# An exponential placed first on ScalarE, and half as many identity products in TensorE's waits

## The chip, the cores and the metric

The kernel runs on one core of one Trainium2 chip. The metric is the device time of one execution, in microseconds (us); less is better. A core has TensorE (PE: matrix products, its weight loads listed apart as PEld), VectorE (DVE), ScalarE (ACT), GpSimd (POOL) and SyncE (SP, which here issues the transfers). They run side by side and wait for each other through semaphores.

## The reference

Attention in two stages with 32 "pack" vectors for each head, then a feed-forward layer with Silu over all heads:

```
q, k, v: (8, 8, 576, 64)   p: (8, 8, 32, 64)      # batch, heads, tokens, width
sm_attn(q, k, v) = softmax(q @ k.T / 8) @ v
p_packed = sm_attn(p, k, v)
x = sm_attn(q, p_packed, p_packed)                # then (4608, 512): tokens x (head, width)
h = x @ w_in                                      # w_in (512, 2048)
out = (h * sigmoid(h)) @ w_out                    # w_out (2048, 512)
```

All is float32.

## The kernel before, in words

The feed-forward layer is computed with the packs inside: since x is (shares of the packs) times (packs), `packs @ w_in` is made first for each batch ("pp" steps), and the shares ("a2") are multiplied with it. A **unit** is one batch and one block of 128 of the 2048 hidden columns: `h` makes its products (line 521), `g` its Silu on ScalarE (539 to 542), `o` the products with w_out (557), summed up in PSUM. To keep precision, most operands are split into a high and a low part and multiplied in three products; the first four units (`u < WHOLE`) use whole float32 values instead.

The early part, until all 64 early units are done, is one list written out by hand, `ORDER`. Each word is a step, and each engine takes its part of the steps strictly in this order (PE, DVE, ACT and SP are scheduled by hand). The words that the change and the prediction touch, for batch 0 (`as0.1` is step `as` of batch 0, second half):

- `W8`: `keep_warm(8)`, line 135: eight 128x128 products of the identity `ident` with itself into a PSUM tile that nobody reads. One float32 product is two instructions on PE, so `W8` shows as x16 in the profile. They stand where PE waits for another engine or for a transfer.
- `k0`, `v0`, `q0`: transfers of the packs and keys (in two pieces), of the values, and of the queries (in two pieces); `wf0` to `wf18`: of chunks of the two weight matrices.
- `ws`, `wz`, `wj`: scaling (ACT, lines 188 and 189), sign (DVE, 193 and 194) and joining (DVE 200, then DVE or POOL 201) of the weights, which arrive as 64-bit integers that hold the bits of a number.
- first attention: `as` scores (PE, line 228), `am` largest value (DVE, 264, 265), `ax` exponentials (ACT, 274), `ar` reciprocals (DVE, 278, 279), `at` transposes (PE, 293), `ay` copies out of PSUM (DVE for the first parity, ACT for the second, 311 and 312), `aa` products with v (PE, 326), `an` (DVE, 336), `ai` (PE 345, ACT copy 349).
- `pp0` packs times w_in (PE, 228), `pu0` its copy (ACT, 486).
- second attention: `aS` scores (PE, 228), `aC` copy (ACT, 370), `aB` transposes (PE, 378), `aM` less the largest (DVE, 407, 408), `aX` exponentials (ACT, 419), `aD` shares (DVE, 428 to 431), `aU` transposes back (PE, 398 and 400), `aF` copy (ACT, 445).
- `h0.0`: the products of the first unit, first half; then `g0.0`, and so on. `as1.0`, `as1.1`, `ac1.1` (ACT, 254), `am1` belong to batch 1; `h2.0` is the third unit.

Both exponentials and Silu run on ScalarE, which loads a table when it goes from one function to the other (`ACT_TABLE_LOAD`); copies and scalings need no load of their own. `two_banks()` gives one of two PSUM tiles, in turn; the tile of the identity products is given up when the next step asks for one. After `ORDER`, a plain loop goes over the rest of the units.

In `ORDER`, the stretch from the start to the first unit reads

```
W8 k0 as0.0 W1 as0.1 am0.0 wf0 wf1 am0.1 ax0.0 ax0.1 ar0 v0 ws0 wz0 W5 at0.0 ay0.0 at0.1 ay0.1 wf2 ws1 ws2 wj0 W15
aa0 an0 W2 ai0 wz2 aj0 q0 W2 pp0 aS0.0 aC0.0 pu0 W2 aS0.1 aB0.0 aC0.1 wj2 pp1 wz1 wj1 wf3 ws3 aM0.0 aX0.0 wf4 ws4
aB0.1 aM0.1 aX0.1 aD0.0 W32 aU0.0 wf5 ws5 wf6 ws6 aD0.1 wz4 aF0.0 W4 h0.0 pu1 k1 g0.0 wz6 aU0.1 aF0.1 wj6 as1.0
```

Of the kernel before, what the change touches and what calls it, by code (L numbers as in the profile page):

```python
# [9 lines left out]
F32 = mybir.dt.float32  # L10
# [4 lines left out]
AF = mybir.ActivationFunctionType  # L15
# [4 lines left out]
P = 128  # L20
# [30 lines left out]


ORDER = """
W8 k0 as0.0 W1 as0.1 am0.0 wf0 wf1 am0.1 ax0.0 ax0.1 ar0 v0 ws0 wz0 W5 at0.0 ay0.0 at0.1 ay0.1 wf2 ws1 ws2 wj0 W15
aa0 an0 W2 ai0 wz2 aj0 q0 W2 pp0 aS0.0 aC0.0 pu0 W2 aS0.1 aB0.0 aC0.1 wj2 pp1 wz1 wj1 wf3 ws3 aM0.0 aX0.0 wf4 ws4
aB0.1 aM0.1 aX0.1 aD0.0 W32 aU0.0 wf5 ws5 wf6 ws6 aD0.1 wz4 aF0.0 W4 h0.0 pu1 k1 g0.0 wz6 aU0.1 aF0.1 wj6 as1.0
ac1.0 wu1 h1.0 g1.0 wf7 wf8 aH0.1 wz5 h0.1 g0.1 h1.1 ws7 v1 wz3 as1.1 wj3 ac1.1 wj5 wj4 g1.1 am1 o0.0 ax1.0 ax1.1
pp3 wz7 wj7 wf9 pp2 pu2 o1.0 at1.0 at1.1 pu3 o0.1 h2.0 h2.1 ws8 g2.0 g2.1 ws9 aL0.1 wz8 o1.1 h3.0 h3.1 wf10 ws10 wj8
o2.0 wz9 aH0.0 wj9 wz10 wj10 g3.0 g3.1 wf11 ws11 o2.1 pp4 aL0.0 o3.0 ay1 aa1 pu4 pl4 h4 wu5 wu10 g4 ar1 an1 ai1 wl1
# [24 lines left out]
def packed_attention_ffn(ctx: ExitStack, tc: tile.TileContext, pkT, qT, v, w_in, w_out, out):  # L84
# [13 lines left out]
    nc = tc.nc  # L98
    ent = ctx.enter_context
    const = ent(tc.tile_pool(name="const", bufs=1))  # L100
# [10 lines left out]
    ident = const.tile([P, P], F32, name="ident")  # L111
# [4 lines left out]

    rest = const.tile([P, NF, 2, 2, REST], F32, name="rest")
    parts = tc.dram_tile((EARLY, 2, P, 2, DM), F32, name="parts")

    made = {}  # L120

# [662 lines left out]
```

## Time and profile before

| | |
|---|---|
| device time, median of 3 runs | 713.53 us (713.42 to 713.99) |
| profiled execution | 713.74 us, span 711.8 us |
| PE busy | 700.6 us (98%), 5126 products |
| DVE, ACT, POOL busy | 332.5 us (47%), 328.3 us (46%), 20.9 us (3%) |
| products of the identity (line 135) | 142 instructions, 19.6 us busy (pipelined, so with overlap) |
| table loads on ACT | 16 under line 539 (20.5 us) and 2 under line 274 up to 60 us, 1283 ns each |
| HBM | 85 GB/s over the span; 356 GB/s in its first fortieth |

The span goes from the first to the last instruction of the execution; the device time has some 2 us more around it. In a line of the timeline the first number is the start in us from the start of the span, the second the time that the group took, then engine, line, operation, the tiles (written <- read), shapes and count; in square brackets stands how long the engine was idle before, and what ended that. In a list of transfers the last number is the median time from issue to landing in us.

### The profile page before, as it was taken

Reading aid. Unit: us, or ns where it says so; the run is one execution under the profiler, and the core shown is the slowest. Engines: PE = TensorE matmul, PEld = TensorE weight load, DVE = VectorE, ACT = ScalarE, POOL = GpSimd, SP = SyncE. Lnnn points to the kernel's source line nnn. Section 1 sums busy time; section 2 is a strip of 40 time slices with the busy share of each in tenths; the row PEclk is TensorE's granted clock in tenths of the full one; section 3 lists DMA queues with packets and bytes.
Section 4 is the critical chain, followed back from the end, with each engine's and each line's share of the span. In section 5 each row is a group of like instructions: output and inputs, shape, how many; then the busy total and the mean of one; then the engine's idle time right before and its main releaser. Section 6 shows DMA issues by size and latency. Waiting matters only on the chain.

```text
span 711.8 us, 12233 instructions
## 1 busy us (share of the span) xinstructions
PE 700.6 (98%) x5126; PEld 570.4 (80%) x5126; DVE 332.5 (47%) x491; ACT 328.3 (46%) x613; POOL 20.9 (3%) x16
## 2 busy tenths in 40 slices
PE   8999999999999999999999999999999999999997
PEld 6756778887868887888878888878878888888886
DVE  3979985854643336331562325533362334622112
ACT  3696867733534425362542625453352532533221
POOL 0112011110000000000000000000000000000000
PEclk9999999999999999999999999999999999999999
DMA  9765572425032140212211122021401210010002
GB/s 356 295 201 196 191 255 101 164 68 192 1 130 82 34 145 1 105 39 87 75 60 56 43 89 75 22 104 36 145 1 60 81 36 1 1 60 1 1 0 75
DMA packets 30870, 65.21 MB, mean 92 GB/s; under 512 B 19296, under 2 KB 19296, under 8 KB 26464
## 3 DMA queue, kind: packets, MB, share of 16 engines
q1 hardware_dynamic: 30720, 64.30, 25.6%
q8 instruction: 41, 0.67, 0.4%
q10 hardware_dynamic: 96, 0.13, 0.1%
q14 instruction: 13, 0.11, 0.0%
HBM read 48.76 MB, written 11.53 MB: 85 GB/s over the span
## 4 chain that ended last, share of the span: by engine, by line
PE 96%; ACT 1%; DVE 1%; SPq 0%; DMA 0%; issue 0%; POOL 0%; ACTq 0%; POOLq 0%; DVEq 0%
PE ps_acc L557 56%; PE ps_two L521 28%; PE ps_two L228 6%; PE ps_two L135 2%; PE ps_two L326 2%; SPq L305 0%; PE ps_acc L228 0%; ACT tm L274 0%; DVE mx L264 0%; ACT L274 0%; DMA tm<-tm 0%; PE ps_acc L326 0%; ACT pw_hi L486 0%; PE ps_acc L293 0%; PE ps_acc L378 0%
## 5 line engine op out<-in xcount | busy, mean ns | idle before, releaser
L557 PE MATMUL ps_acc<-wo_hi,g_hi 128*128 128x512 f32 x560 | 222.5, 397 | 0.0
L557 PE MATMUL ps_acc<-wo_lo,g_hi 128*128 128x512 f32 x560 | 219.1, 391 | 0.0
L557 PE MATMUL ps_acc<-wo_hi,g_lo 128*128 128x512 f32 x560 | 219.0, 391 | 0.0
L547 DVE TENSOR_TENSOR g_lo<-g,g_hi 128x512 fp32r<-128x512 f32 x124 | 89.2, 720 | 256.6 <-ACT g_hi L541 256.5
L539 ACT ACTIVATE g<-ps_two 128x512 f32<-128x512 f32 x124 | 74.4, 600 | 265.6 <-PE ps_two L521 236.7
L521 PE MATMUL ps_two<-a_lo,pw_hi 128*128 128x288 f32 x528 | 155.4, 303 | 0.1
L521 PE MATMUL ps_two<-a_hi,pw_hi 128*128 128x288 f32 x496 | 147.2, 297 | 1.0 <-ACT rest L542 1.0
L521 PE MATMUL ps_two<-a_hi,pw_lo 128*128 128x288 f32 x496 | 145.9, 294 | 0.0
L557 PEld LDWEIGHTS ps_acc<-wo_hi,g_hi 128*128 128x128 f32 x560 | 105.1, 188 | 38.8 <-issue 19.4
L557 PEld LDWEIGHTS ps_acc<-wo_hi,g_lo 128*128 128x128 f32 x560 | 105.1, 188 | 23.6 <-DVE g_lo L547 0.7
L557 PEld LDWEIGHTS ps_acc<-wo_lo,g_hi 128*128 128x128 f32 x560 | 105.2, 188 | 18.1
L521 PEld LDWEIGHTS ps_two<-a_lo,pw_hi 128*128 128x128 f32 x528 | 98.9, 188 | 6.6 <-ACT rest L542 0.8
L521 PEld LDWEIGHTS ps_two<-a_hi,pw_hi 128*128 128x128 f32 x496 | 93.3, 188 | 5.7 <-ACT rest L542 1.3
L521 PEld LDWEIGHTS ps_two<-a_hi,pw_lo 128*128 128x128 f32 x496 | 93.2, 188 | 0.0
L541 ACT ACTIVATE g_hi<-ps_two 128x512 fp32r<-128x512 f32 x124 | 73.6, 593 | 7.8 <-PE ps_acc L557 7.8
L489 DVE TENSOR_TENSOR pw_lo<-ps_two,pw_hi 128x1024 fp32r<-128x1024 f32 x31 | 36.8, 1220 | 9.4 <-ACT pw_hi L486 9.4
L486 ACT CAST pw_hi<-ps_two 128x1024 fp32r<-128x1024 f32 x31 | 30.2, 1017 | 15.9 <-PE ps_two L228 15.9
L228 PE MATMUL ps_two<-win,ppT 64*32 64x512 f32 (+1 forms) x560 | 32.4, 559 | 2.4 <-DVE pw_lo L489 1.6
L542 ACT ACTIVATE rest<-ps_two 128x64 f32<-128x64 f32 (+1 forms) x132 | 30.1, 228 | 0.0
L228 PEld LDWEIGHTS ps_two<-win,ppT 64*32 64x32 f32 x560 | 8.1, 105 | 17.4 <-issue 10.1
L539 ACT ACT_TABLE_LOAD x16 | 20.5, 1283 | 2.0 <-PE ps_two L521 1.9
L135 PE MATMUL ps_two<-ident 128*128 128x128 f32 x142 | 19.6, 296 | 1.4 <-POOL ident masks.py:199 1.4
(114 smaller groups left out, 480.6 us busy)
## 6 DMA issues: line engine op xcount, KB each, us to landing
kvq_t<-in_v SPq DMA_DIRECT2D x8, 1280.0 KB, 6.3
kvq_t<-in_pkT SPq DMA_DIRECT2D x7, 1216.0 KB, 6.3
out<-o SPq DMA_DIRECT2D x16, 512.0 KB, 2.8
kvq_t<-in_qT SPq DMA_DIRECT2D x7, 1152.0 KB, 5.1
w_raw<-in_w_in SPq DMA_DIRECT2D x6, 1024.0 KB, 5.7
win<-in_w_out SPq DMA_DIRECT2D x3, 1024.0 KB, 4.7
w_raw<-in_w_out SPq DMA_DIRECT2D x3, 1024.0 KB, 4.6
tm<-tm SPq DMA_DIRECT2D x56, 40.0 KB, 2.0
```

The source lines that it names most:

```text
L135: nc.tensor.matmul(made["warm"][:, 0, :P], ident, ident, start=True, stop=True)
L228: nc.tensor.matmul(bank(par)[NP * i : NP * i + NP], lhs(r, i), rhs(r, i), start=True, stop=True)
L326: nc.tensor.matmul(self.ps[NP * i : NP * i + NP, par * D : par * D + D], e, vs[:n, c, h * D : h * D + D], start=(c == 0), stop=(c == 4),)
L486: nc.scalar.copy(self.hi, self.ps[:, :, : self.nf * P])
L489: nc.vector.tensor_tensor(self.lo, self.ps[:, :, : self.nf * P], self.hi.bitcast(F32), ALU.subtract)
L521: nc.tensor.matmul(bank, p[:, par, cols], a[:, par], start=(n == 0), stop=(n == len(todo) - 1))
L539: nc.scalar.activation(g, ps[..., :MAIN], AF.Silu)
L541: nc.scalar.activation(g_hi, ps[..., :MAIN], AF.Silu)
L542: nc.scalar.activation(to, ps[..., MAIN:HS], AF.Silu)
L547: nc.vector.tensor_tensor(g_lo[:, c], g[:, c], g_hi[:, c].bitcast(F32), ALU.subtract)
L557: nc.tensor.matmul(bank, g[:, rows], w[:, at], start=(first and n == 0), stop=(last and n + 1 == len(todo)))
```

## The change

A tile `ready` of 128x1 is allocated, and ScalarE takes the exponential of the first column of the identity into it before anything else; no step reads `ready`. In `ORDER` the counts of the nine `W` steps go from 8, 1, 5, 15, 2, 2, 2, 32, 4 (71 products, 142 instructions) to 6, 1, 4, 7, 1, 1, 1, 15, 2 (38 products, 76 instructions). Nothing else in the order moves.

```
 ORDER = """
-W8 k0 as0.0 W1 as0.1 am0.0 wf0 wf1 am0.1 ax0.0 ax0.1 ar0 v0 ws0 wz0 W5 at0.0 ay0.0 at0.1 ay0.1 wf2 ws1 ws2 wj0 W15
-aa0 an0 W2 ai0 wz2 aj0 q0 W2 pp0 aS0.0 aC0.0 pu0 W2 aS0.1 aB0.0 aC0.1 wj2 pp1 wz1 wj1 wf3 ws3 aM0.0 aX0.0 wf4 ws4
-aB0.1 aM0.1 aX0.1 aD0.0 W32 aU0.0 wf5 ws5 wf6 ws6 aD0.1 wz4 aF0.0 W4 h0.0 pu1 k1 g0.0 wz6 aU0.1 aF0.1 wj6 as1.0
+W6 k0 as0.0 W1 as0.1 am0.0 wf0 wf1 am0.1 ax0.0 ax0.1 ar0 v0 ws0 wz0 W4 at0.0 ay0.0 at0.1 ay0.1 wf2 ws1 ws2 wj0 W7
+aa0 an0 W1 ai0 wz2 aj0 q0 W1 pp0 aS0.0 aC0.0 pu0 W1 aS0.1 aB0.0 aC0.1 wj2 pp1 wz1 wj1 wf3 ws3 aM0.0 aX0.0 wf4 ws4
+aB0.1 aM0.1 aX0.1 aD0.0 W15 aU0.0 wf5 ws5 wf6 ws6 aD0.1 wz4 aF0.0 W2 h0.0 pu1 k1 g0.0 wz6 aU0.1 aF0.1 wj6 as1.0
...
     parts = tc.dram_tile((EARLY, 2, P, 2, DM), F32, name="parts")
 
+    ready = const.tile([P, 1], F32, name="ready")
+    nc.scalar.activation(ready, ident[:, :1], AF.Exp)
+
     made = {}
```

## The prediction

> **What bounds the kernel now.** The page comes first: span, busy times, and the chain that ended last.
>
> ```profile
> span 711.8 us, 12233 instructions
> PE 700.6 (98%) x5126; PEld 570.4 (80%) x5126; DVE 332.5 (47%) x491; ACT 328.3 (46%) x613; POOL 20.9 (3%) x16
> ...
> PE 96%; ACT 1%; DVE 1%; SPq 0%; DMA 0%; issue 0%; POOL 0%; ACTq 0%; POOLq 0%; DVEq 0%
> ```
>
> PE is busy nearly always, and the chain lies on it for 96%. But part of that busy time is identity products, which no step reads. The change touches only the first 31 us, so the question is what else holds PE there. That is read from the timeline of PE (start, time taken, in brackets the wait).
>
> ```profile
> 1.36 3.78 PE L135 MATMUL ps_two<-ident 128*128 128x128 f32 x16 [1.36 <-POOL ident masks.py:199]
> 5.07 1.15 PE L228 MATMUL ps_acc<-kvq_t 64*32 64x288 f32 x16
> 6.16 0.49 PE L135 MATMUL ps_two<-ident 128*128 128x128 f32 x2
> 6.57 0.72 PE L228 MATMUL ps_acc<-kvq_t 64*32 64x288 f32 x16
> 7.22 1.38 PE L135 MATMUL ps_two<-ident 128*128 128x128 f32 x10
> 10.54 1.49 PE L293 MATMUL ps_acc<-ident,tm 128*128 128x128 f32 x10 [1.94 <-ACT tm L274]
> 11.87 3.51 PE L135 MATMUL ps_two<-ident 128*128 128x128 f32 x30
> 15.31 1.73 PE L326 MATMUL ps_acc<-kvq_t,tm 128*32 128x64 f32 x80
> ...
> 19.08 0.71 PE L135 MATMUL ps_two<-ident 128*128 128x128 f32 x4
> 19.73 0.66 PE L228 MATMUL ps_acc<-o,ppT 64*32 64x256 f32 x16
> 20.32 0.87 PE L378 MATMUL ps_acc<-ident,tm 128*128 128x128 f32 x6
> ...
> 22.00 7.31 PE L135 MATMUL ps_two<-ident 128*128 128x128 f32 x64
> 29.14 0.38 PE L398 MATMUL ps_acc<-ident,tm 128*128 128x128 f32 x2
> ...
> 30.17 1.16 PE L135 MATMUL ps_two<-ident 128*128 128x128 f32 x8
> 31.48 1.21 PE L521 MATMUL ps_two<-a_lo,pw_hi 128*128 128x288 f32 x4
> ...
> 44.00 2.10 PE L521 MATMUL ps_two<-a_lo,pw_hi 128*128 128x288 f32 x8
> ...
> 54.28 1.09 PE L228 MATMUL ps_two<-win,ppT 64*32 64x512 f32 x16 [0.83 <-DVE win L201]
> ```
>
> An identity product takes 0.24 us at first (3.78/16) and 0.12 later (3.51/30); the scores took 1.15 us and then, the same 16 products, 0.72. So PE runs at half rate until some 6.4 us (the record of the granted clock says 1.00 throughout and does not show it). Where an `L135` row has no wait behind it, the next step went when the identity products let it: only another engine's row tells when it could have gone. These are on ACT and DVE.
>
> ```profile
> 8.36 1.28 ACT L274 ACT_TABLE_LOAD   x1 [8.36 <-DVE nm L265]
> 9.65 0.74 ACT L274 ACTIVATE tm<-ps_acc,nm 128x576 f32<-128x576 f32 x1
> ...
> 10.39 0.73 ACT L274 ACTIVATE tm<-ps_acc,nm 128x576 f32<-128x576 f32 x1
> ...
> 30.81 0.38 ACT L486 COPY pw_hi<-ps_two 128x256 f32<-128x256 f32 x1
> ...
> 43.26 0.62 ACT L486 COPY pw_hi<-ps_two 128x256 f32<-128x256 f32 x2
> ```
>
> ```profile
> 8.97 0.15 DVE L265 TENSOR_SCALAR nm<-mx 128x1 f32<-128x1 f32 x1
> ...
> 14.03 0.28 DVE L312 COPY tm<-ps_acc 64x128 f32<-64x128 f32 x1
> ...
> 21.23 0.96 DVE L407 TENSOR_REDUCE on_tokens<-ps_acc 128x24 f32<-128x768 f32 x1 [0.29 <-PE ps_acc L378]
> ...
> 26.02 0.96 DVE L431 TENSOR_TENSOR tm<-tm,on_tokens 128x768 f32<-128x768 f32 x1
> ...
> 31.30 0.69 DVE L201 CUSTOM_DVE_ANT_0 win<-win 128x1024 uint16<-128x1024 uint16 x1
> ...
> 34.71 1.52 DVE L200 TENSOR_SCALAR win<-win 128x512 int32<-128x512 int32 x1
> 36.26 1.67 DVE L201 CUSTOM_DVE_ANT_0 win<-win 128x1024 uint16<-128x1024 uint16 x1
> 38.80 1.35 DVE L264 TENSOR_REDUCE mx<-tm 128x2 f32<-128x1152 f32 x1 [0.87 <-ACT tm L254]
> ```
>
> Between 21.23 and the end of the join at 37.93 no row of DVE bears a wait: DVE is a second line of work there, as tight as PE. Last, the transfers, whose landings the change does not move: issue rows and times to landing of the two pieces of k, of v, and of the second piece of q.
>
> ```profile
> 0.74 0.88 SPq L141 DMA_DIRECT2D kvq_t<-in_pkT  x2
> ...
> 2.74 0.46 SPq L160 DMA_DIRECT2D kvq_t<-in_v  x1
> ...
> 4.23 0.45 SPq L150 DMA_DIRECT2D o<-in_qT  x1
> ```
>
> ```profile
> kvq_t<-in_pkT SPq DMA_DIRECT2D x1, 640.0 KB, 3.8
> kvq_t<-in_pkT SPq DMA_DIRECT2D x1, 576.0 KB, 4.8
> kvq_t<-in_v SPq DMA_DIRECT2D x1, 1280.0 KB, 9.3
> o<-in_qT SPq DMA_DIRECT2D x1, 512.0 KB, 12.0
> ```
>
> They land at about 4.54, 6.0 (issued near 1.2), 12.04 and 16.23.
>
> **The change part by part.** *W8 to W6, before the first scores.* Twelve cold products end near 4.2; the first keys land at 4.54, so `as0.0` goes at about 4.6 instead of 5.07. It stays 1.50 to `as0.1` (5.07 to 6.57), so that goes at 6.10, just behind the second landing. It then runs about 0.07 of its 0.72 longer, being partly before the rate doubles: 0.40 gained. Ends: 0.47 if the rate doubles as early relative to the work, 0.04 if the whole of `as0.1` runs cold (1.15 for 0.72).
>
> *The table.* ACT does nothing before 8.36, and the identity is there by 1.36, so the early load (1.28) and a 128x1 exponential (below the 0.74 of the wide one) end near 3; the cover is 5 us of idle ACT, and without it they would cost up to 2.0. The first `ax` then starts where the load started: 1.29 earlier (9.65 to 8.36), 1.69 with the 0.40. The second waits for its own `nm` (9.12, now 8.72, and some 0.1 to reach ACT): 8.80 for 10.39, so 1.59 goes on to the scaling of the weights and the copies behind it. The wait of 1.94 on PE shrinks to some 0.8 and so hides W5 to W4.
>
> [...]
>
> *W15 to W7.* The ten transposes end at 10.44 instead of 12.03, fourteen products (1.64) at 12.1. `aa0` needs the last copy of DVE, which ended at 14.31 and now at 12.72, and v (12.04). So it starts at 12.75 for 15.31: 2.56 gained, 0.97 of it from these products, and 0.6 becomes a wait.
>
> *The three W2 to W1.* The first two stand beside DVE's scaling and ACT's copy, which end after them: nothing, between 0 and 0.07 each. Nothing but PE's order and q (16.23) holds `aS0.1`: two products fewer, 0.22 by the 0.65 between 19.08 and 19.73 for four, less the pipeline's part. It goes at 16.95, and `aB0.0` and with it `aM0.0` 2.78 earlier (DVE's idle 0.29 allows 0.22 more).
>
> *W32 to W15.* DVE's shares for the first half end at 26.98, now 24.20. The thirty products start at 19.22 and end at 22.7: PE waits 1.5, and `aU0.0` goes at 24.25 for 29.14, 4.89 earlier.
>
> *W4 to W2.* `h0.0` needs the PSUM tile that `pu1` empties (31.19, now 26.30); four products from 25.28 end before. It goes at 26.35 for 31.48: 5.1 earlier.
>
> *What is late next.* DVE. From `aM0.0` on it is 2.78 earlier, not 5.1, and has no idle time until the join at 37.93, now 35.15. Behind that stands `am1`, which had waited 0.87 for ACT's copy of batch 1's scores; that copy, moved with PE, is now there first. So `am1` goes at 35.15 for 38.80: 3.65. On it hang the exponentials of batch 1, then `pu2` and `pu3` on ACT (43.88, now 40.23), then `h2.0`: PE comes there at 38.9 and waits 1.4. From there PE, ACT and DVE all stand 3.65 earlier, the wait of 0.83 at 54.28 included, and the rest is PE's.
>
> Sum: 0.40 + 1.29 - 0.10 + 0.97 + 0.22 + 0.87 = 3.65. Against the profiled execution (span 711.8, time 713.74) that is 708.2 and 710.1; the median of the runs is 0.2 lower: **709.9**.
>
> **The rivals.** *One more cold window.* If the half us without work before `as0.0` puts off the doubling, `as0.1` keeps only 0.04: 713.5 - 3.3 = 710.2, up to 710.5 if transposes run cold too. For it: the rate doubled only after five us of unbroken work. Against: the work is still unbroken but for 0.5. [...]
>
> *The table load stays where it is* (a load is put ahead of line 274 all the same): 0.40 before the exponentials, copies at 13.91, `aa0` at 13.95 (1.36), then 0.22 and 0.87: 2.45, 711.1. Against: between the exponentials of lines 274 and 419 copies and scalings run without a load.
>
> *DVE is not the bound.* The join at 36.26 took 1.67 where the same form took 0.69 at 31.30, beside additions on POOL, and the shift before it 1.52. If these fall apart, 1.0 of DVE's time goes with the join and by an estimate as much with the shift; past 1.45, PE's 5.1 stays: 708.4. Nothing in the change parts them: both follow DVE.
>
> *Slower.* With these waits the clock falls back to the half rate and stays there. From `h0.0` to `h2.0` PE has 12.5 us of work (31.48 to 44.00); at half rate it takes 25, of which 1.4 lies in the wait: 11.1 lost, 7.5 net, 721. It decides if over 6.5 us of that work run cold (1.4, 3.65, and the 1.4 that a measurement of this kernel tells from no change, 0.2%). Against: the wait of 1.94 at 8.60 left the rate full (products at 0.12 after it), and the longest new one is 1.5.
>
> *Within 0.2%.* A wait behind 54 us takes back over 2.2. No row speaks for one.
>
> **How the numbers follow.** The forecast has 0.64, its own range 709.2 to 710.4 (the 0.04 to 0.47 of the start, 0.2 of the three W2, some 0.3 of v and q landing later). One more cold window 0.14, the table load staying 0.06, DVE not the bound 0.08, within 0.2% 0.05, slower 0.03. The range 708.9 to 711.2 takes in all but half of the DVE case and the last two.
>
> **What would show it.** A table load near 1.4 and none ahead of line 274's first exponential, which starts near 8.0; `aa0` near 12.8 with a wait of half a us before it; `aU0.0` near 24.3 with 1.5 of wait on DVE; `h0.0` near 26.4; `am1` near 35.2 with no idle time on DVE before it; `h2.0` near 40.3 after a new wait on ACT's `pw_hi`. Products of 0.24 after 7 us, or a wait on a transfer ahead of lines 326 or 228, would make it wrong.

## The result, and the profile after

The changed kernel took 717.37 us (median of 4 runs, 716.94 to 717.82) against 713.71 us for the kernel before (4 runs): a ratio of 1.0051, 95% interval 1.0034 to 1.0069. It is slower by half a per cent; 709.9 was predicted. The profiled execution took 716.94 us. Three executions of the kernels below are in the medians but not in the ratios: one of 772.98 us (the kernel before), one of 2406.17 us (the halved products alone) and one of 909.94 us at a granted clock of 0.778 (the weights alone by 32 bytes), which is that kernel's profiled one and is not read.

First the page after: span, busy times, and the chain that ended last.

```profile
span 715.1 us, 12103 instructions
PE 702.2 (98%) x5060; PEld 563.6 (79%) x5060; DVE 332.5 (46%) x491; ACT 328.7 (46%) x614; POOL 21.0 (3%) x16
...
PE 91%; DVE 4%; ACT 2%; DMA 1%; SPq 1%; issue 0%; ACTq 0%; DVEq 0%
```

PE executes 66 products fewer and is busy for 1.6 us more. The timeline says where that isn't: in the first 54 us. (The lines of the file are three further on: 138 is `keep_warm`, 560 the products with w_out.) PE, then ACT, then DVE:

```profile
4.59 1.21 PE L231 MATMUL ps_acc<-kvq_t 64*32 64x288 f32 x16 [0.30 <-DMA kvq_t<-in_pkT]
...
6.16 0.72 PE L231 MATMUL ps_acc<-kvq_t 64*32 64x288 f32 x16
...
12.81 1.73 PE L329 MATMUL ps_acc<-kvq_t,tm 128*32 128x64 f32 x80 [0.80 <-DVE tm L315]
...
24.37 0.41 PE L401 MATMUL ps_acc<-ident,tm 128*128 128x128 f32 x2 [1.29 <-DVE tm L434]
...
26.29 2.26 PE L524 MATMUL ps_two<-a_lo,pw_hi 128*128 128x288 f32 x4
...
40.35 2.10 PE L524 MATMUL ps_two<-a_lo,pw_hi 128*128 128x288 f32 x8
...
50.62 1.09 PE L231 MATMUL ps_two<-win,ppT 64*32 64x512 f32 x16 [0.83 <-DVE win L204]
```

```profile
0.73 1.28 ACT L121 ACT_TABLE_LOAD   x1 [0.73 <-PEq L779]
...
7.96 0.74 ACT L277 ACTIVATE tm<-ps_acc,nm 128x576 f32<-128x576 f32 x1 [5.73 <-DVE nm L268]
...
8.80 0.74 ACT L277 ACTIVATE tm<-ps_acc,nm 128x576 f32<-128x576 f32 x1
...
25.54 0.64 ACT L448 COPY a_lo<-ps_acc 128x576 f32<-128x576 f32 x1 [0.30 <-PE ps_acc L403]
26.07 0.38 ACT L489 COPY pw_hi<-ps_two 128x256 f32<-128x256 f32 x1
```

```profile
33.51 1.68 DVE L204 CUSTOM_DVE_ANT_0 win<-win 128x1024 uint16<-128x1024 uint16 x1
35.15 1.35 DVE L267 TENSOR_REDUCE mx<-tm 128x2 f32<-128x1152 f32 x1
```

Here every step starts within 0.15 of where the prediction put it: `aa0` at 12.81, `aU0.0` at 24.37, `h0.0` at 26.29, `am1` at 35.15 with no idle time on DVE before it, `h2.0` at 40.35. (Two of them do so for another reason than the one predicted; see below.) The product at 54.28 starts at 50.62: 3.66 earlier. But the span is 3.3 longer, so 7.0 were lost behind it. The groups of the products with w_out, before and after (busy time, mean ns of one):

```profile
L557 PE MATMUL ps_acc<-wo_hi,g_hi 128*128 128x512 f32 x560 | 222.5, 397 | 0.0
L557 PE MATMUL ps_acc<-wo_lo,g_hi 128*128 128x512 f32 x560 | 219.1, 391 | 0.0
L557 PE MATMUL ps_acc<-wo_hi,g_lo 128*128 128x512 f32 x560 | 219.0, 391 | 0.0
```

```profile
L560 PE MATMUL ps_acc<-wo_hi,g_hi 128*128 128x512 f32 x560 | 225.2, 402 | 0.0
L560 PE MATMUL ps_acc<-wo_hi,g_lo 128*128 128x512 f32 x560 | 221.5, 396 | 0.1
L560 PE MATMUL ps_acc<-wo_lo,g_hi 128*128 128x512 f32 x560 | 221.2, 395 | 0.0
```

The three sums grow by 7.3 us: 4 to 5 ns on each of 1680 products, whose count and order have not changed. The timeline of PE in the middle of the run, for the same unit before and then after, shows it from start to start:

```profile
380.32 0.39 PE L557 MATMUL ps_acc<-wo_hi,g_lo 128*128 128x512 f32 x1
380.55 0.39 PE L557 MATMUL ps_acc<-wo_hi,g_hi 128*128 128x512 f32 x1
...
382.13 0.39 PE L557 MATMUL ps_acc<-wo_lo,g_hi 128*128 128x512 f32 x1
```

```profile
379.80 0.39 PE L560 MATMUL ps_acc<-wo_hi,g_lo 128*128 128x512 f32 x1
380.03 0.40 PE L560 MATMUL ps_acc<-wo_hi,g_hi 128*128 128x512 f32 x1
...
381.67 0.40 PE L560 MATMUL ps_acc<-wo_lo,g_hi 128*128 128x512 f32 x1
```

Eight steps take 1.81 us before (0.226 each) and 1.87 after (0.234). No row between them bears a wait. The unit starts 0.52 earlier after than before; of the 3.66 at 54 us so much is left at 380, and at the end it has turned into a loss of 3.3.

One thing differs for these products: where their operands lie in SBUF, the memory in which the program allocates these tiles. The new tile `ready` lies in it ahead of the pools of kvq, pw, a2, tmp, small, g and o. It has 4 bytes in each partition and takes 32, so all of these stand 32 bytes further on; the weights `wo_hi` and `wo_lo`, which lie ahead of it, stay. By the programs' lists of allocations `wo_hi` begins at byte 49792 and the first `g_hi` at 192128 before, at 192160 after. The distance was 556 times 256 bytes and is 32 more now.

### The profile page after: what moved, and what is told of

The parts are those of the page before. It is cut to its first block, busy times and chain, and to the rows that moved or that the text cites. A ratio compares the mean times of both kernels' runs of the same rounds, so it can differ in the third digit from the quotient of the medians.

```text
span 715.1 us, 12103 instructions
## 1 busy us (share of the span) xinstructions
PE 702.2 (98%) x5060; PEld 563.6 (79%) x5060; DVE 332.5 (46%) x491; ACT 328.7 (46%) x614; POOL 21.0 (3%) x16
## 4 chain that ended last, share of the span: by engine, by line
PE 91%; DVE 4%; ACT 2%; DMA 1%; SPq 1%; issue 0%; ACTq 0%; DVEq 0%
PE ps_acc L560 56%; PE ps_two L524 27%; PE ps_two L231 6%; SPq L308 1%; PE ps_two L329 1%; DMA w_raw<-in_w_in 1%; DMA kvq_t<-in_pkT 1%; ACT tm L277 0%; PE ps_acc L231 0%; DVE win L204 0%; DVE mx L267 0%; DVE win L203 0%; PE ps_acc L329 0%; DVE tm L411 0%; DVE tm L434 0%
## 5 line engine op out<-in xcount | busy, mean ns | idle before, releaser
L560 PE MATMUL ps_acc<-wo_hi,g_hi 128*128 128x512 f32 x560 | 225.2, 402 | 0.0
L560 PE MATMUL ps_acc<-wo_hi,g_lo 128*128 128x512 f32 x560 | 221.5, 396 | 0.1
L534 ACT CAST g_hi<-rest 128x512 fp32r<-128x512 f32 x16 | 9.9, 622 | 14.6 <-PE ps_acc L560 14.6
```

Of the source, the lines that this page charges most:

```text
L534: nc.scalar.copy(g_hi, g)
L560: nc.tensor.matmul(bank, g[:, rows], w[:, at], start=(first and n == 0), stop=(last and n + 1 == len(todo)))
```

## The experiments

Three theories stood against each other: the place of tiles in SBUF; the clock, or fewer products of the identity, slowing PE to the end; the added instruction on ScalarE. Each ratio below is to the kernel before in the same series of runs, whose medians there were 713.75 to 714.21 us.

**A wider tile.**

```
-    ready = const.tile([P, 1], F32, name="ready")
-    nc.scalar.activation(ready, ident[:, :1], AF.Exp)
+    ready = const.tile([P, 16], F32, name="ready")             # 64 bytes in each partition
+    nc.scalar.activation(ready[:, :1], ident[:, :1], AF.Exp)   # column 0 is written
```

> The change as it is, but the tile of the early exponential is 64 bytes wide in each partition instead of 4, of which one column is used; so every tile behind it in SBUF stands 64 bytes further on than before the change, where the change puts it 32 bytes further on. Theory of the place (tiles at a multiple of 32 but not of 64 bytes make each product with w_out take 5 to 8 ns longer): the 6.9 us lost behind 61 us are gone, products with w_out at 0.227 us from start to start, 713.7 - 3.8 = 709.9 us (709.5 to 710.4). Rival, the clock or the number of identity products (a start with fewer of them leaves PE slower to the end): as the change, 717.4 us. Rival, the added instruction on ScalarE or the shifted instruction stream: 717.4 us too.

Measured: 717.28 us, ratio 1.0040 (1.0026 to 1.0053). The theory as it stood, a multiple of 64 bytes, fell; the two rivals were not yet ruled out. The loss is in the same place: by its page the three groups of products with w_out are 6.7 longer than before (667.3 for 660.6).

**The 32 bytes alone.**

```
# the kernel before, and only
+    pad = const.tile([P, 1], F32, name="pad")
+    nc.gpsimd.memset(pad, 0.0)
```

> The kernel before, with nothing but a tile of 4 bytes in each partition added at the same place (set to zero once by GpSimd, so that it is kept), which moves the tiles behind it by 32 bytes. No early exponential, no product removed. Theory of the place: 713.7 + 6.9 = 720.6 us (719.5 to 721.5), products with w_out at 0.232 to 0.235 us. Rival, the clock or the number of products: 713.7 us. Rival, the instruction on ScalarE: 713.7 us.

Measured: 722.15 us, ratio 1.0104 (1.0088 to 1.0120). Without the exponential and with all identity products, the time grows by 1%: both rivals fall. It is 0.65 above the expected range, and its profiled execution has two losses (the timeline of PE, then the page).

```profile
10.31 1.95 PE L296 MATMUL ps_acc<-ident,tm 128*128 128x128 f32 x10 [1.93 <-ACT tm L277]
12.05 4.73 PE L138 MATMUL ps_two<-ident 128*128 128x128 f32 x30
...
55.67 1.09 PE L231 MATMUL ps_two<-win,ppT 64*32 64x512 f32 x16 [0.81 <-DVE win L204]
```

```profile
L560 PE MATMUL ps_acc<-wo_hi,g_hi 128*128 128x512 f32 x560 | 225.2, 402 | 0.0
L560 PE MATMUL ps_acc<-wo_hi,g_lo 128*128 128x512 f32 x560 | 221.4, 395 | 0.0
```

The three groups are 7.2 longer, as in the change. The other 1.4 were lost at the start (55.67 for 54.28), where the thirty identity products took 4.73 instead of 3.51: PE was at half rate there (granted clock 0.68 from 12 to 16). That is another loss than the one in question; more on it below. The memset is an instruction too; kernels further down that differ in places alone rule out a shifted instruction stream.

**The early exponential alone** (a tile of 64 bytes, all products of before).

> The early exponential alone, into a tile of 64 bytes, with all identity products of before. By the prediction's steps only the table load goes from the path, since the products then set when each next step starts: 713.7 - 1.3 = 712.4 us (712.1 to 712.6). Rival, the exponential itself slows ScalarE or the rest: 713.7 us or more.

Measured: 719.52 us, ratio 1.0071 (1.0057 to 1.0084). The expectation took 64 bytes for harmless and missed. The step itself is there: the transposes that started at 10.54 start at 9.29. Its three groups of products are as long as in the first experiment (667.3, 6.7 more than before), and 714.2 - 1.3 + 6.7 gives 719.6.

**The halved products alone** (no tile, no exponential).

> The halved counts of identity products alone, no early exponential and no tile for it. By the prediction's steps, with the table load still on the path: 0.4 before the exponentials, 1.0 behind them, 0.2 and 0.9: 713.7 - 2.5 = 711.2 us (710.8 to 711.6). Rival, fewer products leave PE slower to the end: 713.7 + 4 us or more.

Measured: 712.17 us, ratio 0.9974 (0.9959 to 0.9989): faster, by some 0.6 less than expected; single executions reach from 710.73 to 715.38. Its products with w_out are as long as before (660.5). In its profiled execution PE stayed at half rate longer at the start (PE timeline; the 16 score products at 6.54 take 1.21, not 0.72):

```profile
6.54 1.21 PE L229 MATMUL ps_acc<-kvq_t 64*32 64x288 f32 x16
...
11.01 2.40 PE L294 MATMUL ps_acc<-ident,tm 128*128 128x128 f32 x10 [1.25 <-ACT tm L275]
```

That is the rival "one more cold window". It is not in the profile of the change, but it is in 4 of the 12 profiled executions with the halved counts: here, and below with everything moved by 32 bytes, with the tile of 128 bytes and with the weights moved by 128. With the same instructions at the start, it came in some executions and not in others.

**The change without a tile.**

```
-    ready = const.tile([P, 1], F32, name="ready")
-    nc.scalar.activation(ready, ident[:, :1], AF.Exp)
+    nc.scalar.activation(rest[:, NF - 1, 1, 1, REST - 1 :], ident[:, :1], AF.Exp)
```

> The change without a tile of its own: the early exponential is written into the last column of the tile rest, which is overwritten much later. No tile moves in SBUF; the halved products and the early table stay. Theory of the place: 713.9 - 3.8 = 710.1 us (709.5 to 710.8), products with w_out at 0.227 us from start to start. Rival, the instruction added on ScalarE or the whole of the change slows the steady part: 717.3 us.

Measured: 709.85 us (709.72 to 710.96), ratio 0.9946 (0.9934 to 0.9959). This is the time that was predicted for the change, and it is faster than both kernels. Its page:

```profile
span 708.1 us, 12103 instructions
...
L559 PE MATMUL ps_acc<-wo_hi,g_lo 128*128 128x512 f32 x560 | 219.0, 391 | 0.1
```

**Which tiles.** From that version on, pools were moved one by one with tiles that are never written, such as

```
+    ent(tc.tile_pool(name="pad_a", bufs=1)).tile([P, 8], F32, name="pad_a")    # 32 bytes
     gp = ent(tc.tile_pool(name="gp", bufs=2))
+    ent(tc.tile_pool(name="pad_b", bufs=1)).tile([P, 120], F32, name="pad_b")  # 480 bytes
     osb = ent(tc.tile_pool(name="osb", bufs=2))
```

All pools by 512 bytes (the change, with `ready` of 128 columns):

> The change with a tile of 512 bytes in each partition for the exponential (one column used), so that all tiles behind it stand 512 bytes further on than before. If what counts is the place within 512 bytes or a divisor of it above 64: 710.1 us as without a tile. If it counts how far the tiles are from those in front of the new one (weights of the second layer), or the place in a longer period: 717 us.

Measured: 710.57 us, ratio 0.9954 (0.9941 to 0.9966). Harmless.

The pool of g by 32 bytes, as in the diff:

> As the version without a tile of its own, but the pool of the g tiles (stationary operand of the products with w_out) is moved by 32 bytes, and the pools behind it by 512; pw, a2 and all in front stay. If the place of g is what counts: products with w_out at 0.232 to 0.235 us in the two units of three whose g is in that pool, so some 4 to 5 us lost: 714 to 715 us. If the place of pw and a2 counts: 710.1 us.

Measured: 716.18 us, ratio 1.0030 (1.0019 to 1.0041): 6.3 more than without the move, and more than expected, since all early units have their g in this pool as well. (`ORDER` makes 32 units, not 64.) The three groups are 5.4 longer (666.0), where the change has 7.3. The units of the second pool, which this kernel moves by 512, come every third time behind `ORDER`. Of two units that follow each other near the end, the first has its g there, the second in the pool moved by 32:

```profile
692.57 0.39 PE L561 MATMUL ps_acc<-wo_hi,g_hi 128*128 128x512 f32 x1
...
695.06 0.40 PE L561 MATMUL ps_acc<-wo_hi,g_lo 128*128 128x512 f32 x1
695.30 0.39 PE L561 MATMUL ps_acc<-wo_hi,g_hi 128*128 128x512 f32 x1
...
697.86 0.40 PE L561 MATMUL ps_acc<-wo_hi,g_lo 128*128 128x512 f32 x1
```

Eleven steps take 2.49 in the first (0.226 each) and 2.56 in the second (0.233), in one execution and with the same instructions. Further ahead the units of the second pool lose a part as well (2.54 in the one at 681.02, 2.50 in the same unit without the move); why is not shown.

pw and a2 by 32 bytes:

> As the version without a tile of its own, but the pools of pw and a2 (operands of the products of a unit) are moved by 32 bytes and the pools behind them by 512; all in front stays. If the place of g alone counts, within 512 bytes: 710.1 us. If the place of pw and a2 counts: 715 to 717 us.

Measured: 709.68 us, ratio 0.9944 (0.9930 to 0.9957). Harmless; but pw and a2, which are multiplied with each other, moved together, so this says nothing on a distance between them.

**Place or distance.** Every tile by 32 bytes, the weights too; then `wo_hi` and `wo_lo` alone by 32:

```
+    const.tile([P, 8], F32, name="pad_a")               # all: ahead of ident
     ident = const.tile([P, P], F32, name="ident")
...
+    const.tile([P, 8], F32, name="pad_a")               # weights alone: ahead of wo_hi,
     wo_hi = const.tile([P, NF, DM], F32R, name="wo_hi")
     wo_lo = const.tile([P, NF, DM], F32R, name="wo_lo")
+    const.tile([P, 120], F32, name="pad_b")             # and 480 bytes behind wo_lo
```

> As the version without a tile of its own, but every tile, from the identity and the weights of the second layer on, is moved by 32 bytes together. If the place of g itself counts: 717 us, as with the change. If what counts is how g lies to the weights of the second layer, with which it is multiplied: 709.9 us.

> As the version without a tile of its own, but only the weights of the second layer, the moving operand of the products with w_out, are moved by 32 bytes; all behind them by 512. If the place of g itself counts: 709.9 us. If how g lies to these weights counts: 716 to 717 us.

Measured: 710.70 us, ratio 0.9951 (0.9936 to 0.9966), with everything moved; 717.41 us, ratio 1.0045 (1.0033 to 1.0058), with the weights alone. g stands 32 bytes off in the first and at a multiple of 512 from its old place in the second: its place doesn't count, its distance to the weights does. Both kernels have the instructions of the version without a tile, so neither an added instruction nor a shifted stream of them is the cause.

**The period.** The change with a tile of 128 and of 256 bytes:

> The change with a tile of 128 bytes in each partition, so that all tiles behind it stand 128 bytes further on. If the period of the place is 128 bytes: 710 us. If it is 256 or 512: 717 us.

> The change with a tile of 256 bytes in each partition, so that all tiles behind it stand 256 bytes further on. If the period of the place is 128 or 256 bytes: 710 us. If it is 512: 717 us.

Measured: 716.95 us, ratio 1.0036 (1.0025 to 1.0048); and 709.99 us, ratio 0.9944 (0.9932 to 0.9955). From the two pages:

```profile
span 715.1 us, 12103 instructions
...
L560 PE MATMUL ps_acc<-wo_hi,g_lo 128*128 128x512 f32 x560 | 221.4, 395 | 0.1
```

```profile
span 708.0 us, 12103 instructions
...
L560 PE MATMUL ps_acc<-wo_hi,g_lo 128*128 128x512 f32 x560 | 219.0, 391 | 0.1
```

**From the other side, and another pair.** The weights alone by 128 bytes; and a2 alone by 128:

> As the version without a tile of its own, but only the weights of the second layer are moved, by 128 bytes; all behind them by 256. If the distance of g to these weights counts, with a period of 256 bytes: 717 us, as with the tile of 128 bytes in front of g. If the direction or the place of the weights matters too: another time. Its profile shows which products lengthen.

> As the version without a tile of its own, but only the a2 tiles, the stationary operand of the products of a unit, are moved by 128 bytes against pw, their moving operand; all behind a2 by 256. If any pair of stationary and moving operand on TensorE suffers from its distance, the some 1500 products of 128x288 lengthen by several ns each as well: 717 us or more. If the loss comes from DVE and ACT, which write g while the products with w_out run, or is special to that pair: 709.9 us, since a2 is written only once for each batch.

Measured: 716.24 us, ratio 1.0031 (1.0018 to 1.0045), for the weights; its products with w_out are as slow as with g moved:

```profile
span 715.2 us, 12103 instructions
...
L561 PE MATMUL ps_acc<-wo_hi,g_lo 128*128 128x512 f32 x560 | 221.4, 395 | 0.1
```

For a2: 709.42 us, ratio 0.9941 (0.9926 to 0.9956), no loss. This one can't tell what it was meant to. The expectation had the operands exchanged (pw is stationary, a2 is moving), which would not matter, but one half of a2 begins 1152 bytes behind the other, and that is 128 beyond a multiple of 256: by moving a2 by 128 the two halves only exchange their parts.

So the loss is shown to hang on the distance between g and the weights: of the moves tried there is none by 0, 256 or 512 bytes or together with the weights, and 6 to 8 us by 32 and 128 on either side and by 64. That fits a period of 256 bytes. Expectation and experiments left open whether PE alone is slower with them or something else that reads or writes g hinders it. The traces before and after settle that. Near the end of both no other engine and no transfer works (windows of before, then after; columns: stretch, sum, busy times of PE, PEld, DVE, ACT and POOL, granted clock, share of the DMA engines, GB/s), and the products are slower all the same:

```profile
702.00:705.00 3.00, 3.00 (x15) 2.49 (x14) 0.00 (x0) 0.00 (x0) 0.00 (x0) 1.00 0.00 0
```

```profile
705.00:708.00 3.00, 3.00 (x15) 2.41 (x14) 0.00 (x0) 0.00 (x0) 0.00 (x0) 1.00 0.00 0
```

```profile
702.17 0.39 PE L557 MATMUL ps_acc<-wo_lo,g_hi 128*128 128x512 f32 x1
...
704.89 0.39 PE L557 MATMUL ps_acc<-wo_lo,g_hi 128*128 128x512 f32 x1
```

```profile
705.32 0.40 PE L560 MATMUL ps_acc<-wo_lo,g_hi 128*128 128x512 f32 x1
...
708.12 0.40 PE L560 MATMUL ps_acc<-wo_lo,g_hi 128*128 128x512 f32 x1
```

Twelve steps take 2.72 before (0.227 each) and 2.80 after (0.233). What works on g and the weights there is PE alone, with its weight loads (busy for 2.49 and 2.41 of the 3.00 us) and its products. By what mechanism the distance slows them is not shown.

## Why the prediction was wrong

Up to the product at 54.28 the times were right: 3.66 gained there for 3.65. Start: 0.41 at `as0.1` for 0.40, in an execution without the cold window. Table: the first `ax` at 7.96 and the second at 8.80, as worked out; the load runs in idle time, from 0.73 to 2.01, earlier than the 1.4 that was expected. W15 to W7: `aa0` at 12.81 for 12.75. The three W2: `aS0.1` at 16.98 for 16.95. W32: `aU0.0` at 24.37 for 24.25, after a wait of 1.29 on DVE. What is late next was DVE, and `am1` fell on 35.15 as predicted.

Two times are luck. W4: `h0.0` at 26.29 for 26.35 was to wait for the PSUM tile that `pu1` empties, but it starts while that copy still runs (26.07, 0.38 long), right behind the copy of `a_lo` (25.54, 0.64 long), which it reads; its PSUM tile is the one of the identity products. And `h2.0` at 40.35 was to come after a new wait on ACT's `pw_hi`, but its row bears no wait: PE came late itself, as told below.

The step that failed is the last: "From there PE, ACT and DVE all stand 3.65 earlier, the wait of 0.83 at 54.28 included, and the rest is PE's". It took the rate of PE's products for given. The allocation of `ready` was costed as an instruction alone; the place that it takes in SBUF was put at nothing without a reason, and "Within 0.2%" looked behind 54 us for a wait only. The missing term is +7.3 us by the three groups of the two pages, and with it the sum is right: 713.7 - 3.65 + 7.3 = 717.4. The version without the tile, where the term is nothing, took the 709.9 that was predicted.

The rival "slower" had the right sign and the wrong mechanism. The half rate did come back behind the wait of 1.29, though it did not stay, against the argument that no wait was longer than one which had done no harm. The windows of the changed kernel (columns as above):

```profile
24.00:28.00 4.00, 3.48 (x14) 2.50 (x15) 3.83 (x9) 3.43 (x6) 0.00 (x0) 0.77 1.03 427
28.00:32.00 4.00, 4.00 (x30) 2.30 (x29) 3.90 (x10) 2.39 (x6) 0.21 (x1) 0.80 0.52 216
```

The granted clock is 0.50 from 27 to 29. At this half rate for (0.23 + 0.20) x 4 x 2 = 3.4 us, the four products at 26.29 took 2.26 instead of 1.21. The loss fell into the time that PE had in hand, as the rival's working had it. The profiled execution with the tile of 256 bytes has the same start at the full rate (granted clock 1.00), and there `h2.0` does wait:

```profile
39.90 2.21 PE L524 MATMUL ps_two<-a_lo,pw_hi 128*128 128x288 f32 x8 [0.54 <-ACT pw_hi L489]
...
50.52 1.09 PE L231 MATMUL ps_two<-win,ppT 64*32 64x512 f32 x16 [0.81 <-DVE win L204]
```

So the half rate put off `h2.0` by some 0.4, and nothing of that was left at 50.62.

The argument itself took one execution for a rule. The kernel with the 32 bytes alone has the start of the kernel before, and in its profiled execution a wait of 1.93 was followed by the half rate, where 1.94 had left the rate full. With the halved counts the clock fell after waits on DVE of 1.00 (the pool of g by 32) to 1.55 (the halved products alone), and not after 1.28 (the tile of 128 bytes). The length of the wait alone does not decide; what else does is not shown.

## What to carry to other kernels

A new tile is a change of everything allocated behind it. Before costing an added tile at nothing, compare where the operands of the busiest instruction lie before and after, above all the stationary against the moving one on TensorE: here a multiple of 256 bytes between them was worth 1%, more than the whole change. Use a spare column of an existing tile, or make the new one 256 bytes wide (both were run here), or allocate it last (not run). Where a change to the start moves the time, look whether the steady part still runs at its old rate, from start to start, before looking for waits. And take the clock of one profiled execution for one draw: look at several before calling a wait harmless.

## What the runs showed of the hardware that was not expected

- Products of 128x512 in float32r with g and w_out at a multiple of 256 bytes from each other followed each other at 0.226 us in the unit shown, and at 0.234 with 32 bytes more; over all 1680 of them that is 4 to 5 ns each.
- TensorE fell back to half rate in six profiled executions after waits of 1.00 to 1.93 (for 3.4 us in the changed kernel, by granted clocks of 0.77 and 0.80 in the two windows of 4 us), and kept the full rate in others after waits of 1.28 and 1.94.
